# Larger pieces of K work, and a new order for the last heads, in a one-token attention and feed-forward kernel

## The chip, the cores and the metric

The kernel runs on one core of a Trainium2 chip. The metric is the device time of one execution in microseconds (us); lower is better. The six runs of the kernel before lie within 0.33% of each other, so differences of under about 1 us need several runs. The record marks every run used here as fast, that is, undisturbed. The engines are named as in the profile: PE multiplies matrices (PEld is its weight load), DVE is VectorE, ACT is ScalarE, POOL is GpSimd, SP issues nearly all loads. PSUM is the memory into which PE writes its sums. The granted clock is the share of PE's full clock that the profile says PE was given.

## The reference, cut to what matters

```python
x  = A_x                                   # 4 x 1 x 640: one token of four sequences
xn = layernorm(x)
q  = xn @ wq                               # 32 heads of 192
k, v = last W = 2048 positions of the caches, 32 heads     # 4 x 32 x 2048 x 192 each, bf16
o  = softmax(q . k * 192**-0.5) . v
out = x + o @ wo + (silu(xn @ w1) * (xn @ w3)) @ w2
```

Per head the kernel reads 3,072 KB of K and as much of V, once. All inputs together are 222.96 MB, and there is hardly any arithmetic per byte.

## The kernel before

Per head, DVE multiplies K with q in four quarters (`mult`), PE adds up six blocks of 32 columns with identity matmuls (`adder`), and DVE reduces the rest to scores (`reduce_quarter`). Then comes the chain of the head: maximum per partition (`lmax`), transposition on PE, maximum per sequence (`gmax`), broadcast on PE (`bc`), exponential on ACT, and `z`, the exponentials spread for the value product. `pv` is the value product, `ge_sum` gathers it into `po`, `ge_tot` the sum of the exponentials.

```python
def mult(u):                       # u counts quarters: head h = u // 4
    pr = ppool.tile([P, JQ, Dh], BF16, tag="pr")          # 4 buffers
    nc.vector.tensor_tensor(out=pr[:], in0=kts[h][:, g*JQ:(g+1)*JQ, :], in1=<q, repeated>, op=ALU.mult)
def adder(u):
    ps = ps_add.tile([P, JQ, DD], FP32, tag="ps")         # PSUM, 2 buffers, one quarter each
    for kk in range(NK):
        nc.tensor.matmul(ps[:], lhsT=idb[:], rhs=pr[:, :, kk*DD:(kk+1)*DD], start=..., stop=...)
def reduce_quarter(u):
    nc.vector.tensor_reduce(out=scs[h][:, g*JQ:(g+1)*JQ], in_=pss.pop(u)[:], axis=AX.X, op=ALU.add)
...
mt = ps_m.tile([P, P + 1], FP32, tag="mt")                # a PSUM tile of its own for the chain
po = ps_po.tile([P, Dh + 1], FP32, name="po")             # another for ge_sum and ge_tot
...
ends = {H - 2: (NU - 1, NU), H - 1: (NU + 3, NU + 4)}     # slots of pv and ge_sum of the last heads
for h in range(H):
    u0, ul = h * GQ, h * GQ + GQ - 1
    ...
    for u in range(u0, ul + 1):
        add(u, 1, mult, u); add(u + 1, 2, adder, u); add(u + 1, 8, reduce_quarter, u)
    add(ul + 1, 9, chain_lmax, h)
    add(ul + 2, 3, chain_tr, h);  add(ul + 2, 4, chain_gmax, h)
    add(ul + 3, 3, chain_bc, h);  add(ul + 3, 4, chain_z, h)
    add(ul + 4, 5, ge_tot, h)
```

`add(slot, phase, ...)` fixes the order in which each engine gets its instructions. Engines take them in this order, and an instruction that waits holds up those behind it (in a_undo30 below, adder matmuls on PE stand behind a wait of 1.58 us). In before, a head's chain is thus laced into the multiplications of the next head.

Of the kernel before, what the change touches and what calls it, by code (L numbers as in the profile page):

```python
# [10 lines left out]
FP32 = mybir.dt.float32  # L11
# [39 lines left out]
def kernel(  # L51
# [16 lines left out]
    PBUFS: int = 4,  # L68
# [43 lines left out]
    ps_m = ctx.enter_context(tc.tile_pool(name="ps_m", bufs=1, space=MemoryType.PSUM))  # L112
    ps_t = ctx.enter_context(tc.tile_pool(name="ps_t", bufs=1, space=MemoryType.PSUM))
# [7 lines left out]
    wos, o_sbs, rsums, rts, chs, oTs = {}, {}, {}, {}, {}, {}  # L121
# [36 lines left out]
    ones_ff = const.tile([1, 1], FP32, name="ones_ff")  # L158
    nc.vector.memset(ones_ff[:], 1.0)
# [4 lines left out]
    nc.vector.tensor_copy(out=mask_b[:], in_=mask_f[:])  # L164
# [32 lines left out]
    xnT_ps = ps_t.tile([P, KC, B], BF16, tag="t")  # L197
# [11 lines left out]
    xm = ppool.tile([B, 2, PH, 2], BF16, tag="pr", name="xm")  # L209
    nc.gpsimd.memset(xm[:], 0.0)  # L210
    for i in range(2):
        nc.vector.tensor_copy(out=xm[:, i, :, i], in_=xn[:, KM * P:LB])
    xe = ppool.tile([B, 3 + LE, LF], BF16, tag="pr", name="xe")
    nc.gpsimd.memset(xe[:], 0.0)
    for g in range(2):
        b0 = LB + g * 2 * LP
        nc.vector.tensor_copy(out=xe[:, 0:2, g * CT:g * CT + LP].rearrange("b s (e i) -> b s e i", i=LI),
                              in_=xn[:, b0:b0 + 2 * LP].rearrange("b (i e s) -> b s e i", e=LE, s=2))
    nc.vector.tensor_copy(out=xe[:, 2, 0:LP].rearrange("b (e i) -> b e i", i=LI),
                          in_=xn[:, LB + 4 * LP:LB + 5 * LP].rearrange("b (i e) -> b e i", e=LE))  # L220
    for e in range(LE):
        nc.vector.tensor_copy(out=xe[:, 3 + e, CT + e * LI:CT + (e + 1) * LI], in_=xn[:, LB + 5 * LP:D])
    NX = KM + 2
    xw_ps = ps_t.tile([P, NX + 3 + LE, B], BF16, tag="t", name="xw_ps")
    for kc in range(KM):
        nc.tensor.transpose(out=xw_ps[:, kc, :], in_=xn[:, kc:KM * P:KM], identity=idb[0:B, 0:B])
    for i in range(2):
        nc.tensor.transpose(out=xw_ps[:, KM + i, :], in_=xm[:, i].rearrange("b r h -> b (r h)"), identity=idb[0:B, 0:B])
    for i in range(3 + LE):
        nc.tensor.transpose(out=xw_ps[0:LF, NX + i, :], in_=xe[:, i, :], identity=idb[0:B, 0:B])  # L230
    xw = const.tile([P, NX, NREP, B], BF16, name="xw")
    nc.vector.tensor_copy(out=xw[:], in_=xw_ps[:, 0:NX, :].unsqueeze(2).to_broadcast([P, NX, NREP, B]))
    xl = const.tile([LF, 3 + LE, NREP, B], BF16, name="xl")
    nc.vector.tensor_copy(out=xl[:], in_=xw_ps[0:LF, NX:, :].unsqueeze(2).to_broadcast([LF, 3 + LE, NREP, B]))


    qbc = const.tile([P, H * Dh], BF16, name="qbc")
    for c0 in range(0, NQ, 6):
        qps = [pool.tile([P, QC], FP32, tag=tag, name="qps")
               for pool, tag in ((ps_add, "ps"), (ps_add, "ps"), (ps_o, "o_ps"), (ps_o, "o_ps"), (ps_m, "mt"), (ps_t, "t"))]  # L240
        for kc in range(KC):
            for i, qp in enumerate(qps):
                nc.tensor.matmul(qp[:], lhsT=xnT[:, kc].rearrange("p a b -> p (a b)"),  # L243
                                 rhs=wq_rows[kc][:, (c0 + i) * QC:(c0 + i + 1) * QC],
                                 start=(kc == 0), stop=(kc == KC - 1))
# [24 lines left out]
    po = ps_po.tile([P, Dh + 1], FP32, name="po")  # L270
# [3 lines left out]
    def mult(u):  # L274
        h, g = u // GQ, u % GQ
        pr = ppool.tile([P, JQ, Dh], BF16, tag="pr")
        nc.vector.tensor_tensor(out=pr[:], in0=kts[h][:, g * JQ:(g + 1) * JQ, :],  # L277
                                in1=qbc[:, h * Dh:(h + 1) * Dh].unsqueeze(1).to_broadcast([P, JQ, Dh]),
                                op=ALU.mult)
        prs[u] = pr  # L280
        if g == GQ - 1:
            kts.pop(h)

    def adder(u):
        ps = ps_add.tile([P, JQ, DD], FP32, tag="ps")
        pr = prs.pop(u)
        for kk in range(NK):
            nc.tensor.matmul(ps[:], lhsT=idb[:], rhs=pr[:, :, kk * DD:(kk + 1) * DD],  # L288
                             start=(kk == 0), stop=(kk == NK - 1))
        pss[u] = ps  # L290

    def reduce_quarter(u):
# [3 lines left out]
        nc.vector.tensor_reduce(out=scs[h][:, g * JQ:(g + 1) * JQ], in_=pss.pop(u)[:], axis=AX.X, op=ALU.add)  # L296
# [6 lines left out]
    def chain_tr(h):  # L303
        mt = ps_m.tile([P, P + 1], FP32, tag="mt")
# [269 lines left out]
```

## Time and profile before

| | before |
|---|---|
| time, median | 525.69 us (six runs, 525.56 to 527.29; of the first three, 525.79) |
| span of the profile | 523.8 us |
| loads | 222.96 MB, 99.2% of 16 engines' span |
| busy PE, DVE | 69%, 65% |

The first fence is from the page of the kernel before: the engines' busy time, then 40 equal slices of the span (busy share in tenths, and GB/s), then the queue that carries the loads.

```profile
span 523.8 us, 4820 instructions
...
PE 361.8 (69%) x2336; PEld 75.9 (14%) x1643; DVE 340.9 (65%) x413; ACT 55.8 (11%) x176; POOL 5.6 (1%) x12
...
DMA  9999999999999999999999999999999999999996
GB/s 389 422 443 425 433 431 432 428 433 432 430 435 428 437 418 446 424 437 426 434 434 429 432 434 429 435 427 435 425 437 434 427 437 431 430 434 425 441 418 275
...
q1 hardware_dynamic: 11868, 222.96, 99.2%
```

DMA is at 9 in every slice but the last. The slices carry about 431 GB/s. The Trainium skill, "DMA: Bandwidth & Descriptors", section "Where 436 GB/s comes from", gives 435.2 GB/s as the ceiling of the ports of on-chip memory, and the trace stays just under it. The same section expects loads from HBM, as these are, to be held to about 358 GB/s; the 431 GB/s measured here, with one core loading, are above that, so the measurement decides. The loads' 99.2% is 519.6 us: a floor.

Next, three groups of the kernel before, by line and shape: count, then busy us and mean ns of one, then the engine's idle time just before them and what ended it.

```profile
L277 DVE TENSOR_TENSOR pr<-kt,qbc 128x3072 bf16<-128x3072 bf16 x128 | 223.5, 1746 | 104.0 <-DMA kt<-in_A_k_cache_dram 104.0
...
L296 DVE TENSOR_REDUCE sc<-ps 128x16 f32<-128x512 f32 x128 | 87.1, 681 | 2.7 <-PE ps L288 2.6
...
L332 DVE TENSOR_TENSOR z<-ex,mask_b 128x256 bf16<-128x256 bf16 x32 | 13.5, 423 | 38.6 <-ACT ex L324 38.6
```

DVE waited 104.0 us for K to land: it was ahead of the loads. Last, the timeline of the end of before: start us, duration, engine, line, operation; in brackets the idle time before it and its releaser.

```profile
496.99 1.76 DVE L277 TENSOR_TENSOR pr<-kt,qbc 128x3072 bf16<-128x3072 bf16 x1 [4.05 <-DMA kt<-in_A_k_cache_dram]
...
505.17 0.43 DVE L332 TENSOR_TENSOR z<-ex,mask_b 128x256 bf16<-128x256 bf16 x1 [1.44 <-ACT ex L324]
...
506.11 1.75 DVE L277 TENSOR_TENSOR pr<-kt,qbc 128x3072 bf16<-128x3072 bf16 x1
...
510.13 0.22 DVE L300 TENSOR_REDUCE lmax<-sc 128x1 f32<-128x64 f32 x1
...
513.30 2.71 PE L340 MATMUL o_ps<-vt,z 128*8 128x384 bf16 x32 [0.24 <-DVE z L332]
...
516.05 0.48 ACT L343 COPY o_sb<-o_ps 128x384 f32<-128x384 f32 x1 [3.27 <-PE o_ps L340]
...
519.21 0.98 PE L264 MATMUL acc<-wo_t,oT 128*4 128x320 bf16 x12 [0.47 <-DMA wo_t<-in_A_wo_dram]
...
520.38 0.71 PE L264 MATMUL acc<-w,hT 128*4 128x320 bf16 x8 [0.19 <-DMA w<-in_B_w_dram]
```

Head 31's K lands at 496.99 us, and its first multiplication starts at once. Its fourth waits behind head 30's `z` (505.17). The chain's `lmax` is at 510.13, the value product runs from 513.30 to 516.01. The output projection then waits 0.47 us for its weights and the last eight matmuls wait 0.19 us for w2: the loads end last.

### The profile page before, as it was taken

The numbers are of one execution on the slowest core, as the hardware profiler recorded it, in microseconds if no ns is written. First come the engines' busy times: TensorE is split into PE (matmuls) and PEld (weight loads), VectorE is DVE, ScalarE is ACT, GpSimd is POOL, SyncE is SP. The second block draws the span as 40 slices with busy tenths as digits, with TensorE's granted clock in tenths as the row PEclk, the third lists the DMA queues.
The fourth block names the chain that finished last, engine by engine and source line by source line (L and its number), as shares of the span: only waits on it lengthen the run. The fifth ranks groups of instructions, "written<-read, shape, count | busy, mean of one in ns | idle before, by whom it ended". The sixth has DMA issues, their size and how long they took to land.

```text
span 523.8 us, 4820 instructions
## 1 busy us (share of the span) xinstructions
PE 361.8 (69%) x2336; PEld 75.9 (14%) x1643; DVE 340.9 (65%) x413; ACT 55.8 (11%) x176; POOL 5.6 (1%) x12
## 2 busy tenths in 40 slices
PE   0965866887668776667547768586686876675685
PEld 0100111121111111111111111111111111111122
DVE  3268853687656767577646877466667766667671
ACT  2111111111001110101100111001101110011111
POOL 4000000000000000000000000000000000000000
PEclk9979886898878998789997988889878898889988
DMA  9999999999999999999999999999999999999996
GB/s 389 422 443 425 433 431 432 428 433 432 430 435 428 437 418 446 424 437 426 434 434 429 432 434 429 435 427 435 425 437 434 427 437 431 430 434 425 441 418 275
DMA packets 11904, 223.26 MB, mean 426 GB/s; under 512 B 1332, under 2 KB 1608, under 8 KB 3052
## 3 DMA queue, kind: packets, MB, share of 16 engines
q1 hardware_dynamic: 11868, 222.96, 99.2%
q8 instruction: 15, 0.25, 0.2%
q14 instruction: 5, 0.04, 0.0%
q10 hardware_dynamic: 16, 0.01, 0.0%
HBM read 222.96 MB, written 0.01 MB: 426 GB/s over the span
## 4 chain that ended last, share of the span: by engine, by line
DMA 60%; PE 20%; DVE 15%; ACT 3%; issue 1%; SPq 1%
DMA kt<-in_A_k_cache_dram 44%; PE ps L288 11%; DMA w<-in_B_w_dram 11%; DVE pr L277 10%; DMA vt<-in_A_v_cache_dram 5%; PE po L361 4%; PE qps L243 3%; DVE sc L296 2%; ACT ex L324 1%; DVE z L332 1%; DMA x_sb<-in_A_x_dram 1%; PE mt L318 1%; ACT L324 0%; ACT negm L321 0%; PE mt L305 0%
## 5 line engine op out<-in xcount | busy, mean ns | idle before, releaser
L288 PE MATMUL ps<-pr,idb 128*128 128x512 bf16 x768 | 214.7, 422 | 137.6 <-DVE pr L277 137.5
L277 DVE TENSOR_TENSOR pr<-kt,qbc 128x3072 bf16<-128x3072 bf16 x128 | 223.5, 1746 | 104.0 <-DMA kt<-in_A_k_cache_dram 104.0
L296 DVE TENSOR_REDUCE sc<-ps 128x16 f32<-128x512 f32 x128 | 87.1, 681 | 2.7 <-PE ps L288 2.6
L340 PE MATMUL o_ps<-vt,z 128*8 128x384 bf16 x1024 | 60.5, 380 | 0.2 <-DVE z L332 0.2
L361 PE MATMUL po<-o_sb,sel_w 128*32 128x192 f32 x128 | 49.2, 518 | 0.6 <-ACT o_sb L343 0.6
L340 PEld LDWEIGHTS <-z 128*8 128x8 bf16 x1024 | 26.2, 95 | 98.8 <-issue 89.2
L332 DVE TENSOR_TENSOR z<-ex,mask_b 128x256 bf16<-128x256 bf16 x32 | 13.5, 423 | 38.6 <-ACT ex L324 38.6
L343 ACT COPY o_sb<-o_ps 128x384 f32<-128x384 f32 x32 | 15.3, 478 | 196.9 <-PE o_ps L340 196.9
L313 ACT ACTIVATE gneg<-gmax 1x128 f32<-1x128 f32 x32 | 9.8, 308 | 162.8 <-DVE gmax L310 162.8
L305 PEld LDWEIGHTS mt<-idf,lmax 128*1 128x1 f32 x32 | 3.2, 101 | 127.5 <-issue 125.5
L361 PEld LDWEIGHTS po<-o_sb,sel_w 128*32 128x32 f32 x128 | 13.8, 130 | 29.4 <-issue 27.9
L288 PEld LDWEIGHTS <-idb 128*128 128x128 bf16 x124 | 12.0, 97 | 39.3 <-issue 32.8
L318 PEld LDWEIGHTS mt<-ones_ff,gneg 1*128 1x128 f32 x64 | 9.6, 186 | 47.1 <-issue 43.7
L243 PE MATMUL qps<-wt,xnT 128*128 128x512 bf16 x59 | 14.9, 412 | 0.1
L318 PE MATMUL mt<-ones_ff,gneg 1*128 1x1 f32 x64 | 12.3, 259 | 0.7 <-ACT gneg L313 0.7
L321 ACT COPY negm<-mt 128x1 f32<-128x1 f32 x32 | 5.1, 159 | 70.4 <-PE mt L318 70.4
L310 DVE TENSOR_REDUCE gmax<-mt 1x4 f32<-1x128 f32 x32 | 8.8, 274 | 5.8 <-PE mt L305 5.8
L348 PEld LDWEIGHTS po<-rsum,tot_w 128*32 128x32 f32 x64 | 4.4, 108 | 51.5 <-ACT ex L324 35.4
L249 DVE CAST qbc<-qps 128x512 bf16<-128x512 f32 x6 | 3.8, 684 | 11.7 <-PE qps L243 11.7
L324 ACT ACTIVATE ex<-sc,negm 128x64 bf16<-128x64 f32 x32 | 11.1, 348 | 1.0
L305 PE MATMUL mt<-idf,lmax 128*1 128x128 f32 x32 | 10.9, 340 | 0.0
L199 PE MATMUL xnT_ps<-idb,xn 4*128 4x4 bf16 x5 | 0.4, 178 | 13.4 <-DVE xn L194 13.4
(74 smaller groups left out, 84.4 us busy)
## 6 DMA issues: line engine op xcount, KB each, us to landing
kt<-in_A_k_cache_dram SPq DMA_DIRECT2D x32, 3072.0 KB, 19.1
vt<-in_A_v_cache_dram SPq DMA_DIRECT2D x32, 3072.0 KB, 25.5
wo_t<-in_A_wo_dram SPq DMA_DIRECT2D x8, 960.0 KB, 20.7
wt<-in_A_wq_dram SPq DMA_DIRECT2D x2, 3072.0 KB
w<-in_B_w_dram SPq DMA_DIRECT2D x1, 1920.0 KB
wt<-in_A_wq_dram SPq DMA_DIRECT2D x1, 1536.0 KB, 19.5
w<-in_B_w_dram SPq DMA_DIRECT2D x1, 1536.0 KB
w<-in_B_w_dram SPq DMA_DIRECT2D x2, 640.0 KB
```

What stands on the lines that cost most here:

```text
L243: nc.tensor.matmul(qp[:], lhsT=xnT[:, kc].rearrange("p a b -> p (a b)"), rhs=wq_rows[kc][:, (c0 + i) * QC:(c0 + i + 1) * QC], start=(kc == ...
L277: nc.vector.tensor_tensor(out=pr[:], in0=kts[h][:, g * JQ:(g + 1) * JQ, :], in1=qbc[:, h * Dh:(h + 1) * Dh].unsqueeze(1).to_broadcast([P, ...
L288: nc.tensor.matmul(ps[:], lhsT=idb[:], rhs=pr[:, :, kk * DD:(kk + 1) * DD], start=(kk == 0), stop=(kk == NK - 1))
L296: nc.vector.tensor_reduce(out=scs[h][:, g * JQ:(g + 1) * JQ], in_=pss.pop(u)[:], axis=AX.X, op=ALU.add)
L305: nc.tensor.transpose(out=mt[0:1, 0:P], in_=chs[h][0][:], identity=idf[:])
L313: nc.scalar.activation(out=gneg[:], in_=gmax[:].unsqueeze(1).to_broadcast([1, PB, B]), func=ACTF.Copy, scale=-SCALE)
L318: nc.tensor.matmul(mt[:, P:P + 1], lhsT=gneg[:].rearrange("o p b -> o (p b)"), rhs=ones_ff[:], start=True, stop=True)
L324: nc.scalar.activation(out=ex[:], in_=scs.pop(h)[:], func=ACTF.Exp, bias=negm[:, 0:1], scale=SCALE, accum_out=rsum[:])
L332: nc.vector.tensor_tensor(out=z[:], in0=ex[:].unsqueeze(2).to_broadcast([P, NJ, B]), in1=mask_b[:].unsqueeze(1).to_broadcast([P, NJ, B]), ...
L340: nc.tensor.matmul(o_ps[c * CT:c * CT + 2 * B, :], lhsT=z[:, 2 * jj:2 * jj + 2, :], rhs=vt[:, 2 * jj:2 * jj + 2, :], start=(jj < 4), stop= ...
L343: nc.scalar.copy(out=o_sb[:], in_=o_ps[:])
L361: nc.tensor.matmul(po[sl, 0:Dh], lhsT=sel_w[:, par].rearrange("p a b -> p (a b)"), rhs=o_sb[:, par * Dh:(par + 1) * Dh].rearrange("p (r i) ...
```

## The change

The intent: fewer and larger instructions (half heads for heads 0 to 30, quarters only for head 31), and at the end the work of heads 29 and 30 out of the way before head 31 begins, so that head 31's chain is short. The totals of the exponentials are taken once per four heads. To make room in PSUM for pairs of quarters, `mt` and `po` move into one tile. Preparations for w1 move to GpSimd and to later. The core of the diff:

```diff
+    po_mt = ps_po.tile([P, Dh + 1 + P + 1], FP32, name="po_mt")
+    po, mt = po_mt[:, 0:Dh + 1], po_mt[:, Dh + 1:]
+    def mult(u, n):                      # n quarters at once
+        if u % 2 == 0:
+            prs[u] = ppool.tile([P, 2 * JQ, Dh], BF16, tag="pr", name="pr")   # 2 buffers
...
+    def adder(u, n):
+        if u % 2 == 0:
+            pss[u] = ps_add.tile([P, 2, JQ, DD], FP32, tag="ps", name="ps")   # a pair of quarters
...
-    def ge_tot(h):
-        nc.tensor.matmul(po[sl, Dh:Dh + 1], lhsT=<tot_w>, rhs=rsums.pop(h)[:], ...)
+    def ge_mask(hg):  ...  nc.vector.tensor_tensor(out=rw[:], in0=<tot_w>, in1=<four sums>, op=ALU.mult)
+    def ge_tot(hg):   ...  nc.tensor.matmul(po[:, Dh:Dh + 1], lhsT=<rw>, rhs=ones_ff[:], ...)
...
-    ends = {H - 2: (NU - 1, NU), H - 1: (NU + 3, NU + 4)}
+    ends = {H - 3: (NU - 5, NU - 4.9), H - 2: (NU - 1, NU), H - 1: (NU + 3, NU + 4)}
...
+        n = 2 if h < H - 1 else 1
+        for u in range(u0, ul + 1, n):
+            s = u + n if h != H - 2 else u + 1
+            add(u, 1, mult, u, n); add(s, 2, adder, u, n); add(s, 8, reduce_d, u, n)
+        a, b, c = (ul + 1, ul + 2, ul + 3) if h != H - 2 else (ul, ul + 0.1, ul + 0.2)
+        add(a, 9, chain_lmax, h)
+        add(b, 3, chain_tr, h);  add(b, 4, chain_gmax, h)
+        add(c, 3, chain_bc, h);  add(c, 4, chain_z, h)
         if h % HG == HG - 1:
+            add(ul + 4, 4, ge_mask, h // HG)
+            add(ul + 4, 5, ge_tot, h // HG)       # on PE: ahead of pv of head 31
```

The order of the loads is the same in both kernels.

More of the change, by code (lines that the diff above doesn't have):

```diff
@@ L67 @@
     VBUFS: int = 3,
-    PBUFS: int = 4,
+    PBUFS: int = 2,
     L: int = 8,
@@ L111 @@
     ps_o = ctx.enter_context(tc.tile_pool(name="ps_o", bufs=2, space=MemoryType.PSUM))
-    ps_m = ctx.enter_context(tc.tile_pool(name="ps_m", bufs=1, space=MemoryType.PSUM))
-    ps_t = ctx.enter_context(tc.tile_pool(name="ps_t", bufs=1, space=MemoryType.PSUM))
     ps_po = ctx.enter_context(tc.tile_pool(name="ps_po", bufs=1, space=MemoryType.PSUM))
@@ L120 @@
     kts, vts, prs, pss, scs, exs, zs = {}, {}, {}, {}, {}, {}, {}
-    wos, o_sbs, rsums, rts, chs, oTs = {}, {}, {}, {}, {}, {}
+    wos, o_sbs, rsums, rws, rts, chs, oTs = {}, {}, {}, {}, {}, {}, {}
     def load_k(h):
@@ L157 @@
     make_identity(nc, idf[:])
-    ones_ff = const.tile([1, 1], FP32, name="ones_ff")
-    nc.vector.memset(ones_ff[:], 1.0)
+    ones_ff = const.tile([P, 1], FP32, name="ones_ff")
+    nc.gpsimd.memset(ones_ff[:], 1.0)
     mask_f = const.tile([P, B], FP32, name="mask_f")
@@ L163 @@
     mask_b = const.tile([P, B], BF16, name="mask_b")
-    nc.vector.tensor_copy(out=mask_b[:], in_=mask_f[:])
+    nc.gpsimd.tensor_copy(out=mask_b[:], in_=mask_f[:])
     rows = const.tile([P, 2 * B], FP32, name="rows")
@@ L170 @@
     tot_w = head.tile([P, NREP, B], FP32, name="tot_w")
-    nc.vector.tensor_copy(out=tot_w[:], in_=mask_f[:].unsqueeze(1).to_broadcast([P, NREP, B]))
+    nc.gpsimd.tensor_copy(out=tot_w[:], in_=mask_f[:].unsqueeze(1).to_broadcast([P, NREP, B]))
     sel_w = const.tile([P, 2, NREP, B], FP32, name="sel_w")
     for par in range(2):
-        nc.vector.tensor_copy(out=sel_w[:, par], in_=rows[:, par * B:(par + 1) * B].unsqueeze(1).to_broadcast([P, NREP, B]))
+        nc.gpsimd.tensor_copy(out=sel_w[:, par], in_=rows[:, par * B:(par + 1) * B].unsqueeze(1).to_broadcast([P, NREP, B]))
     xf = ppool.tile([B, D], FP32, tag="pr")
@@ L194 @@
     nc.vector.tensor_scalar_mul(out=xn[:], in0=xc[:], scalar1=rstd[:, 0:1])
-    xnT_ps = ps_t.tile([P, KC, B], BF16, tag="t")
+    xnT_ps = ps_add.tile([P, KC, B], BF16, tag="ps")
     for kc in range(KC):
@@ L208 @@
     assert D - LB == 5 * LP + LI and F % LE == 0
-    xm = ppool.tile([B, 2, PH, 2], BF16, tag="pr", name="xm")
-    nc.gpsimd.memset(xm[:], 0.0)
-    for i in range(2):
-        nc.vector.tensor_copy(out=xm[:, i, :, i], in_=xn[:, KM * P:LB])
-    xe = ppool.tile([B, 3 + LE, LF], BF16, tag="pr", name="xe")
-    nc.gpsimd.memset(xe[:], 0.0)
-    for g in range(2):
-        b0 = LB + g * 2 * LP
-        nc.vector.tensor_copy(out=xe[:, 0:2, g * CT:g * CT + LP].rearrange("b s (e i) -> b s e i", i=LI),
-                              in_=xn[:, b0:b0 + 2 * LP].rearrange("b (i e s) -> b s e i", e=LE, s=2))
@@ L219 @@
-    nc.vector.tensor_copy(out=xe[:, 2, 0:LP].rearrange("b (e i) -> b e i", i=LI),
-                          in_=xn[:, LB + 4 * LP:LB + 5 * LP].rearrange("b (i e) -> b e i", e=LE))
-    for e in range(LE):
-        nc.vector.tensor_copy(out=xe[:, 3 + e, CT + e * LI:CT + (e + 1) * LI], in_=xn[:, LB + 5 * LP:D])
-    NX = KM + 2
-    xw_ps = ps_t.tile([P, NX + 3 + LE, B], BF16, tag="t", name="xw_ps")
-    for kc in range(KM):
-        nc.tensor.transpose(out=xw_ps[:, kc, :], in_=xn[:, kc:KM * P:KM], identity=idb[0:B, 0:B])
@@ L227 @@
-    for i in range(2):
-        nc.tensor.transpose(out=xw_ps[:, KM + i, :], in_=xm[:, i].rearrange("b r h -> b (r h)"), identity=idb[0:B, 0:B])
-    for i in range(3 + LE):
-        nc.tensor.transpose(out=xw_ps[0:LF, NX + i, :], in_=xe[:, i, :], identity=idb[0:B, 0:B])
-    xw = const.tile([P, NX, NREP, B], BF16, name="xw")
-    nc.vector.tensor_copy(out=xw[:], in_=xw_ps[:, 0:NX, :].unsqueeze(2).to_broadcast([P, NX, NREP, B]))
-    xl = const.tile([LF, 3 + LE, NREP, B], BF16, name="xl")
-    nc.vector.tensor_copy(out=xl[:], in_=xw_ps[0:LF, NX:, :].unsqueeze(2).to_broadcast([LF, 3 + LE, NREP, B]))
@@ L237 @@
     qbc = const.tile([P, H * Dh], BF16, name="qbc")
     for c0 in range(0, NQ, 6):
-        qps = [pool.tile([P, QC], FP32, tag=tag, name="qps")
-               for pool, tag in ((ps_add, "ps"), (ps_add, "ps"), (ps_o, "o_ps"), (ps_o, "o_ps"), (ps_m, "mt"), (ps_t, "t"))]
+        pairs = [ps_add.tile([P, 2, QC], FP32, tag="ps", name="qps") for _ in range(2)]
+        qps = [pair[:, i, :] for pair in pairs for i in range(2)]
+        qps += [ps_o.tile([P, QC], FP32, tag="o_ps", name="qps")[:] for _ in range(2)]
@@ L241 @@
         for kc in range(KC):
             for i, qp in enumerate(qps):
-                nc.tensor.matmul(qp[:], lhsT=xnT[:, kc].rearrange("p a b -> p (a b)"),
+                nc.tensor.matmul(qp, lhsT=xnT[:, kc].rearrange("p a b -> p (a b)"),
                                  rhs=wq_rows[kc][:, (c0 + i) * QC:(c0 + i + 1) * QC],
@@ L248 @@
             if i % 2:
-                nc.vector.tensor_copy(out=dst, in_=qp[:])
+                nc.vector.tensor_copy(out=dst, in_=qp)
             else:
-                nc.scalar.copy(out=dst, in_=qp[:])
+                nc.scalar.copy(out=dst, in_=qp)
     o_banks = []
@@ L268, in acc_add, with reduce_d @@
             acc_half(i, lhsT, rhs, last=last)
-    po = ps_po.tile([P, Dh + 1], FP32, name="po")
+    po_mt = ps_po.tile([P, Dh + 1 + P + 1], FP32, name="po_mt")
+    po, mt = po_mt[:, 0:Dh + 1], po_mt[:, Dh + 1:]
     def x_add(i):
         acc_half(i, idb[0:B, 0:B], x_sb, first=True)
-    def mult(u):
+    def mult(u, n):
         h, g = u // GQ, u % GQ
-        pr = ppool.tile([P, JQ, Dh], BF16, tag="pr")
-        nc.vector.tensor_tensor(out=pr[:], in0=kts[h][:, g * JQ:(g + 1) * JQ, :],
-                                in1=qbc[:, h * Dh:(h + 1) * Dh].unsqueeze(1).to_broadcast([P, JQ, Dh]),
-                                op=ALU.mult)
-        prs[u] = pr
-        if g == GQ - 1:
-            kts.pop(h)
-    def adder(u):
-        ps = ps_add.tile([P, JQ, DD], FP32, tag="ps")
-        pr = prs.pop(u)
-        for kk in range(NK):
-            nc.tensor.matmul(ps[:], lhsT=idb[:], rhs=pr[:, :, kk * DD:(kk + 1) * DD],
-                             start=(kk == 0), stop=(kk == NK - 1))
-        pss[u] = ps
-    def reduce_quarter(u):
+        if u % 2 == 0:
+            prs[u] = ppool.tile([P, 2 * JQ, Dh], BF16, tag="pr", name="pr")
+        i = (u % 2) * JQ
+        nc.vector.tensor_tensor(out=prs[u - u % 2][:, i:i + n * JQ, :], in0=kts[h][:, g * JQ:(g + n) * JQ, :],
+                                in1=qbc[:, h * Dh:(h + 1) * Dh].unsqueeze(1).to_broadcast([P, n * JQ, Dh]),
+                                op=ALU.mult)
+    def adder(u, n):
+        if u % 2 == 0:
+            pss[u] = ps_add.tile([P, 2, JQ, DD], FP32, tag="ps", name="ps")
+        ps, pr = pss[u - u % 2], prs[u - u % 2]
+        for i in range(u % 2, u % 2 + n):
+            for kk in range(NK):
+                nc.tensor.matmul(ps[:, i], lhsT=idb[:], rhs=pr[:, i * JQ:(i + 1) * JQ, kk * DD:(kk + 1) * DD],
+                                 start=(kk == 0), stop=(kk == NK - 1))
+    def reduce_d(u, n):
         h, g = u // GQ, u % GQ
@@ L295, in reduce_quarter @@
             scs[h] = small.tile([P, NJ], FP32, tag="sc", name="sc")
-        nc.vector.tensor_reduce(out=scs[h][:, g * JQ:(g + 1) * JQ], in_=pss.pop(u)[:], axis=AX.X, op=ALU.add)
+        nc.vector.tensor_reduce(out=scs[h][:, g * JQ:(g + n) * JQ],
+                                in_=pss[u - u % 2][:, u % 2:u % 2 + n].rearrange("p i j d -> p (i j) d"),
+                                axis=AX.X, op=ALU.add)
     def chain_lmax(h):
@@ L303, in chain_tr @@
     def chain_tr(h):
-        mt = ps_m.tile([P, P + 1], FP32, tag="mt")
         nc.tensor.transpose(out=mt[0:1, 0:P], in_=chs[h][0][:], identity=idf[:])
-        chs[h].append(mt)
     def chain_gmax(h):
         gmax = small.tile([1, B], FP32, tag="gmax")
-        nc.vector.tensor_reduce(out=gmax[:], in_=chs[h][1][0:1, 0:P].rearrange("o (p b) -> o b p", b=B),
+        nc.vector.tensor_reduce(out=gmax[:], in_=mt[0:1, 0:P].rearrange("o (p b) -> o b p", b=B),
                                 axis=AX.X, op=ALU.max)
@@ L316, in chain_bc @@
     def chain_bc(h):
-        lmax, mt, gneg = chs[h]
-        nc.tensor.matmul(mt[:, P:P + 1], lhsT=gneg[:].rearrange("o p b -> o (p b)"), rhs=ones_ff[:],
+        lmax, gneg = chs.pop(h)
+        nc.tensor.matmul(mt[:, P:P + 1], lhsT=gneg[:].rearrange("o p b -> o (p b)"), rhs=ones_ff[0:1, :],
                          start=True, stop=True)
@@ L321, in chain_bc @@
         nc.scalar.copy(out=negm[:], in_=mt[:, P:P + 1])
-        rsum = small.tile([P, 1], FP32, tag="rsum", bufs=4)
+        if h % HG == 0:
+            rsums[h // HG] = small.tile([P, HG], FP32, tag="rsum", bufs=2, name="rsum")
         ex = small.tile([P, NJ], BF16, tag="ex")
         nc.scalar.activation(out=ex[:], in_=scs.pop(h)[:], func=ACTF.Exp, bias=negm[:, 0:1], scale=SCALE,
-                             accum_out=rsum[:])
-        rsums[h] = rsum
+                             accum_out=rsums[h // HG][:, h % HG:h % HG + 1])
         exs[h] = ex
@@ L344, in pv, with ge_mask, ge_tot @@
         o_sbs[h] = o_sb
-    def ge_tot(h):
-        sl = slice((h % HG) * CT, (h % HG + 1) * CT)
-        nc.tensor.matmul(po[sl, Dh:Dh + 1], lhsT=tot_w[:].rearrange("p a b -> p (a b)"), rhs=rsums.pop(h)[:],
+    def ge_mask(hg):
+        rw = small.tile([P, HG, CT], FP32, tag="rw", bufs=1, name="rw")
+        nc.vector.tensor_tensor(out=rw[:], in0=tot_w[:].rearrange("p a b -> p (a b)").unsqueeze(1).to_broadcast([P, HG, CT]),
+                                in1=rsums.pop(hg)[:].unsqueeze(2).to_broadcast([P, HG, CT]), op=ALU.mult)
+        rws[hg] = rw
+    def ge_tot(hg):
+        nc.tensor.matmul(po[:, Dh:Dh + 1], lhsT=rws.pop(hg)[:].rearrange("p h c -> p (h c)"), rhs=ones_ff[:],
                          start=True, stop=True)
-        chs.pop(h)
     def ge_rec(hg):
@@ L382, with w1_rows, w1_x @@
     ffn = {}
+    NX = KM + 2
+    xw = const.tile([P, NX, NREP, B], BF16, name="xw")
+    xl = const.tile([LF, 3 + LE, NREP, B], BF16, name="xl")
+    xs = {}
+    def w1_rows():
+        xm = small.tile([B, 2, PH, 2], BF16, tag="xm", bufs=1, name="xm")
+        nc.gpsimd.memset(xm[:], 0.0)
+        for i in range(2):
+            nc.gpsimd.tensor_copy(out=xm[:, i, :, i], in_=xn[:, KM * P:LB])
+        xe = small.tile([B, 3 + LE, LF], BF16, tag="xe", bufs=1, name="xe")
+        nc.gpsimd.memset(xe[:], 0.0)
+        for g in range(2):
+            b0 = LB + g * 2 * LP
+            nc.gpsimd.tensor_copy(out=xe[:, 0:2, g * CT:g * CT + LP].rearrange("b s (e i) -> b s e i", i=LI),
+                                  in_=xn[:, b0:b0 + 2 * LP].rearrange("b (i e s) -> b s e i", e=LE, s=2))
+        nc.gpsimd.tensor_copy(out=xe[:, 2, 0:LP].rearrange("b (e i) -> b e i", i=LI),
+                              in_=xn[:, LB + 4 * LP:LB + 5 * LP].rearrange("b (i e) -> b e i", e=LE))
+        for e in range(LE):
+            nc.gpsimd.tensor_copy(out=xe[:, 3 + e, CT + e * LI:CT + (e + 1) * LI], in_=xn[:, LB + 5 * LP:D])
+        xs.update(m=xm, e=xe)
+    def w1_x():
+        xm, xe = xs["m"], xs["e"]
+        xw_ps = ps_add.tile([P, NX + 3 + LE, B], BF16, tag="ps", name="xw_ps")
+        for kc in range(KM):
+            nc.tensor.transpose(out=xw_ps[:, kc, :], in_=xn[:, kc:KM * P:KM], identity=idb[0:B, 0:B])
+        for i in range(2):
+            nc.tensor.transpose(out=xw_ps[:, KM + i, :], in_=xm[:, i].rearrange("b r h -> b (r h)"), identity=idb[0:B, 0:B])
+        for i in range(3 + LE):
+            nc.tensor.transpose(out=xw_ps[0:LF, NX + i, :], in_=xe[:, i, :], identity=idb[0:B, 0:B])
+        nc.vector.tensor_copy(out=xw[:], in_=xw_ps[:, 0:NX, :].unsqueeze(2).to_broadcast([P, NX, NREP, B]))
+        nc.vector.tensor_copy(out=xl[:], in_=xw_ps[0:LF, NX:, :].unsqueeze(2).to_broadcast([LF, 3 + LE, NREP, B]))
     FM, FH = KM * F, KM * F + F // 2
@@ L408, in w1_in @@
         wt, we = ffn["w1"], ffn["w1e"]
-        ps = ffn["ps"] = ps_t.tile([P, FW], FP32, tag="t", name="f_ps")
+        ps = ffn["ps"] = ps_add.tile([P, FW], FP32, tag="ps", name="f_ps")
         def mm(w, lhsT, rhs, c0=0, start=False, stop=False):
@@ L442, in w3_in @@
     def w3_in():
-        ffn["ps"] = ps_t.tile([P, FW], FP32, tag="t", name="f_ps")
+        ffn["ps"] = ps_add.tile([P, FW], FP32, tag="ps", name="f_ps")
         for kc in range(KC):
@@ L485 @@
             add(u0 + 2, 0, load_v, h)
-        for u in range(u0, ul + 1):
-            add(u, 1, mult, u)
-            add(u + 1, 2, adder, u)
-            add(u + 1, 8, reduce_quarter, u)
-        add(ul + 1, 9, chain_lmax, h)
-        add(ul + 2, 3, chain_tr, h)
-        add(ul + 2, 4, chain_gmax, h)
-        add(ul + 3, 3, chain_bc, h)
-        add(ul + 3, 4, chain_z, h)
-        add(ul + 4, 5, ge_tot, h)
+        n = 2 if h < H - 1 else 1
+        for u in range(u0, ul + 1, n):
+            s = u + n if h != H - 2 else u + 1
+            add(u, 1, mult, u, n)
+            add(s, 2, adder, u, n)
+            add(s, 8, reduce_d, u, n)
+        a, b, c = (ul + 1, ul + 2, ul + 3) if h != H - 2 else (ul, ul + 0.1, ul + 0.2)
+        add(a, 9, chain_lmax, h)
+        add(b, 3, chain_tr, h)
+        add(b, 4, chain_gmax, h)
+        add(c, 3, chain_bc, h)
+        add(c, 4, chain_z, h)
         if h % HG == HG - 1:
+            add(ul + 4, 4, ge_mask, h // HG)
+            add(ul + 4, 5, ge_tot, h // HG)
             add(ul + 4, 9, ge_rec, h // HG)
@@ L511 @@
         add(4 + 2 * n, 1, w1_low, n)
+    add(5, 0, w1_rows)
+    add(9, 7, w1_x)
     add(13, 7, w1_in)
```

## The prediction

> **What bounds the kernel now.** The load queue. The page's queue table gives queue q1 99.2% of 16 engines' span: 519.6 of 523.8 us for 222.96 MB, all of which must be read. The slices show DMA at 9 in every slice but the last, while PE is busy 69% and VectorE 65%. The Trainium skill, "DMA: Bandwidth & Descriptors", section "Where 436 GB/s comes from", puts the ceiling at 435.2 GB/s; the slices here show about 431, so the trace agrees and hardly any rate is left to win.
>
> The chain of waits for the last 40 us says the same: V load from 465.17 to 489.66, then the last w2 chunks, issued from 489.7 to 497.3 us, landing at 520.34; then eight acc matmuls (0.76 us), the cast (0.47 us) and the store, to 523.8. Everything is queued by 497.3 us, so from there the end is set by bytes alone.
>
> **What the change does to each engine.**
> - VectorE: 31 heads use two multiplications of 6144 columns instead of four of 3072 (1746 ns each), and two reductions instead of four (681 ns each). The work per element stays; 62 starts of each kind go. Small VectorE operations here take 0.14 to 0.2 us, so I estimate 0.05 to 0.1 us saved per start: 6 to 12 us of 341. Eight mask products are added (about 0.3 us each, estimated from the 128x256 z product at 0.42), 2.4 us. About 1 us of w1 row copies goes to GpSimd.
> - PE: the totals go from 64 matmul records (7.1 us) to 16: about 5 us of 362. Adder and value matmuls stay.
> - Head: the w1 transposes (about 1 us) move behind the q product, which starts about 1 us earlier. The first V load, issued at 26.2 us when a wq buffer frees, may go out earlier, but 14.2 MB (33 us at 431 GB/s) are queued ahead of it: no gain.
> - Tail: head 30's chain and head 29's value product go ahead of head 31's multiplications. In before, head 31's fourth multiplication waits until 506.1 us behind head 30's z at 505.2. Head 31's compute should end 1 to 3 us earlier (its o_sb copy was at 516.05). But the last projection already waited 0.47 us for wo_t, and the last acc matmuls for w2.
>
> **On the critical path:** nothing of it, within about 0.2 us. K loads may go out some us earlier or later, but when K is issued at 477.99 us, the K before it still lands at 482.4 and V at 489.7: over 10 us of queue is in hand.
>
> **Predicted time:** 525.6 us against 525.79; range 524.5 to 527.0. Faster by over 2%: 0.01; within 2%: 0.98; slower by over 2%: 0.01.
>
> **What would show each step right.** Queue q1 still about 519.6 us of engine time and DMA 9 throughout; the last w2 landing within 0.5 us of 520.3, the rest after it again about 3.5 us; VectorE busy 328 to 338 us; head 31's o_sb copy at 513 to 515.5 us, followed by longer PE waits on wo_t and w2; first q matmul near 14 us instead of 15.15.
>
> **What would make it wrong.** A stretch where the queue runs dry: the w1 and w3 products now borrow an adder buffer, and GpSimd writes what the w1 transposes read, so PE could stop for a while in the first 110 us; a K or V load issued over 10 us late costs the excess one for one. Or a final chain of head 31 that ends after 520.3 us: its totals now pass a mask product after the exponential.

## The result, and the profile after

The changed kernel takes 533.45 us (median of six runs, 531.49 to 534.12), against 525.69 us. The ratio is 1.0135, 95% interval 1.0113 to 1.0157: 1.35% slower. That is within the 2% to which the prediction gave 0.98, but far outside its range, which ended at 527.0 us. Ratios here and below are the mean time of one kernel's fast runs over that of the other's of the same rounds, so not quite the ratio of the medians quoted.

The same lines of the page of the changed kernel:

```profile
span 530.1 us, 4584 instructions
...
PE 364.1 (69%) x2288; PEld 65.7 (12%) x1534; DVE 334.0 (63%) x284; ACT 55.9 (11%) x176; POOL 7.5 (1%) x25
...
DMA  9999999999999999999999999999999999999991
GB/s 386 430 430 430 437 428 428 435 430 431 431 430 436 433 428 434 430 432 433 433 430 432 430 433 427 436 432 431 430 433 426 436 430 436 434 424 439 426 421 72
...
q1 hardware_dynamic: 11868, 222.96, 98.1%
```

98.1% of 530.1 us is 520.0 us: the loads take what they took. Only the last slice lost: 72 GB/s instead of 275. For the w2 chunks, the profile says how long after its issue a load landed:

```profile
DMA to landing us min/median/max: 23.8/27.2/30.6
```

The last two are issued at 489.64 and 496.9 us and land 30.6 and 23.8 us later, at 520.2 and 520.7; in before it was 520.3 and 520.8. The queue never ran dry, and PE did not wait for w2 at all. The time is lost after the loads. The groups of the changed kernel, by line and shape:

```profile
L251 DVE TENSOR_TENSOR pr<-kt,qbc 128x6144 bf16<-128x6144 bf16 x62 | 207.1, 3341 | 28.9 <-DMA kt<-in_A_k_cache_dram 28.9
L268 DVE TENSOR_REDUCE sc<-ps 128x32 f32<-128x1024 f32 x62 | 75.5, 1217 | 11.8 <-PE ps L261 11.8
...
L304 DVE TENSOR_TENSOR z<-ex,mask_b 128x256 bf16<-128x256 bf16 x32 | 13.5, 422 | 82.6 <-ACT ex L297 82.6
```

VectorE's busy time fell as intended, from 340.9 to 334.0 us. But it waited for K only 28.9 us instead of 104.0, and `z` waited for the exponential 82.6 us instead of 38.6. It does less work and is less ahead of the loads. That alone costs nothing: in a_undo30_mt_tot_ps below, which is as fast as before, the same two waits are 46.3 and 75.0 us. Here is the end of the changed kernel, as a timeline:

```profile
481.43 0.54 SPq L123 DMA_DIRECT2D kt<-in_A_k_cache_dram  x1
...
486.19 2.76 PE L261 MATMUL ps<-pr,idb 128*128 128x512 bf16 x12 [0.57 <-DVE pr L251]
...
490.44 3.33 DVE L251 TENSOR_TENSOR pr<-kt,qbc 128x6144 bf16<-128x6144 bf16 x1
...
493.83 4.45 PE L261 MATMUL ps<-pr,idb 128*128 128x512 bf16 x12 [2.48 <-DVE pr L251]
...
498.32 1.22 DVE L268 TENSOR_REDUCE sc<-ps 128x32 f32<-128x1024 f32 x1 [4.21 <-PE ps L261]
499.58 0.22 DVE L274 TENSOR_REDUCE lmax<-sc 128x1 f32<-128x64 f32 x1
...
500.68 1.52 PE L337 MATMUL po_mt<-o_sb,sel_w 128*32 128x192 f32 x4 [0.46 <-DVE gmax L282]
...
503.20 0.42 DVE L304 TENSOR_TENSOR z<-ex,mask_b 128x256 bf16<-128x256 bf16 x1 [2.68 <-ACT ex L297]
503.55 3.42 DVE L251 TENSOR_TENSOR pr<-kt,qbc 128x3072 bf16<-128x3072 bf16 x2
...
515.63 0.22 DVE L274 TENSOR_REDUCE lmax<-sc 128x1 f32<-128x64 f32 x1
...
519.09 0.55 PE L325 MATMUL po_mt<-ones_ff,rw 128*128 128x1 f32 x2 [1.47 <-DVE rw L320]
...
519.57 2.73 PE L312 MATMUL o_ps<-vt,z 128*8 128x384 bf16 x32
...
522.35 0.48 ACT L315 COPY o_sb<-o_ps 128x384 f32<-128x384 f32 x1 [4.07 <-PE o_ps L312]
...
526.72 0.71 PE L235 MATMUL acc<-w,hT 128*4 128x320 bf16 x8
```

The first line is the issue of head 31's K. The view of that line and time gives its landing:

```profile
DMA to landing us min/median/max: 15.5/15.5/15.5
```

So head 31's K was there at 496.9 us, but its first multiplication starts at 503.55. Before it come head 30's second half (490.44) with its 12 adder matmuls (493.83, 4.45 us), their reduction (498.32), and the whole chain of head 30 from `lmax` (499.58) to `z` (503.20), with the `ge_sum` of head 29 (500.68) in the middle of it on PE. Meanwhile DVE mostly waits. Part of this lateness is the granted clock: the 12 adder matmuls of head 30's first half took 2.76 us (486.19), those of its second half 4.45, with a granted clock of 0.71 between 495 and 500 us. No run holds the clock fixed, so what these 1.7 us are worth is not shown. The last matmuls with w2 come at 526.72 us. The account of the two profiles, from the lines shown:

| piece | before | after | difference |
|---|---|---|---|
| start of head 31's multiplications | 496.99 | 503.55 | +6.56 |
| from there to `lmax` of head 31 | 13.14 | 12.08 | -1.06 |
| from `lmax` to the end of the value product | 5.88 | 6.67 | +0.79 |
| from there to the end of the span | 7.79 | 7.80 | +0.01 |
| sum | | | +6.30 (530.1 - 523.8) |

So 6.6 us of wait came in, only 1.1 us came back because head 30's chain is no longer laced into head 31 (its value product, at 511.99, still is), and 0.8 us is the totals: in before they were done while `z` was computed, now a mask product after `z` and their matmul both stand ahead of the value product. The profiled run is one of the faster ones of the changed kernel (531.97 us); the difference of the medians is 7.8 us.

### The profile page after: what moved, and what is told of

It reads as the page before. It is cut to its first block, busy times and chain, and to the rows that moved or that the text cites. A ratio compares the mean times of both kernels' runs of the same rounds, so it can differ in the third digit from the quotient of the medians.

```text
span 530.1 us, 4584 instructions
## 1 busy us (share of the span) xinstructions
PE 364.1 (69%) x2288; PEld 65.7 (12%) x1534; DVE 334.0 (63%) x284; ACT 55.9 (11%) x176; POOL 7.5 (1%) x25
## 3 DMA queue, kind: packets, MB, share of 16 engines
q1 hardware_dynamic: 11868, 222.96, 98.1%
## 4 chain that ended last, share of the span: by engine, by line
DMA 51%; DVE 27%; PE 18%; ACT 1%; issue 1%; SPq 0%
DMA kt<-in_A_k_cache_dram 43%; DVE pr L251 18%; PE ps L261 9%; DMA w<-in_B_w_dram 5%; DVE sc L268 5%; DMA wt<-in_A_wq_dram 4%; PE po_mt L337 3%; PE o_ps L312 2%; PE qps L214 1%; PE po_mt L278 1%; DVE gmax L282 1%; PE acc L235 1%; DVE z L304 1%; DVE lmax L274 1%; ACT ex L297 1%
## 5 line engine op out<-in xcount | busy, mean ns | idle before, releaser
L261 PE MATMUL ps<-pr,idb 128*128 128x512 bf16 x768 | 220.2, 447 | 18.7 <-DVE pr L251 16.8
L251 DVE TENSOR_TENSOR pr<-kt,qbc 128x6144 bf16<-128x6144 bf16 (+1 forms) x66 | 214.0, 3245 | 28.9 <-DMA kt<-in_A_k_cache_dram 28.9
L268 DVE TENSOR_REDUCE sc<-ps 128x32 f32<-128x1024 f32 (+1 forms) x66 | 78.2, 1185 | 14.5 <-PE ps L261 14.5
L278 PE MATMUL po_mt<-idf,lmax 128*1 128x128 f32 x32 | 9.6, 301 | 94.5 <-DVE lmax L274 94.5
L304 DVE TENSOR_TENSOR z<-ex,mask_b 128x256 bf16<-128x256 bf16 x32 | 13.5, 422 | 82.6 <-ACT ex L297 82.6
L337 PE MATMUL po_mt<-o_sb,sel_w 128*32 128x192 f32 x128 | 48.7, 515 | 14.1 <-DVE gmax L282 12.5
L312 PE MATMUL o_ps<-vt,z 128*8 128x384 bf16 x1024 | 51.5, 336 | 0.0
L290 PEld LDWEIGHTS po_mt<-ones_ff,gneg 1*128 1x128 f32 x64 | 9.4, 182 | 106.7 <-issue 105.8
L282 DVE TENSOR_REDUCE gmax<-po_mt 1x4 f32<-1x128 f32 x32 | 8.9, 279 | 16.4 <-PE po_mt L278 16.4
L337 PEld LDWEIGHTS po_mt<-o_sb,sel_w 128*32 128x32 f32 x128 | 14.0, 130 | 35.3 <-issue 29.5
L290 PE MATMUL po_mt<-ones_ff,gneg 1*128 1x1 f32 x64 | 12.1, 256 | 0.7 <-ACT gneg L285 0.7
```

What stands on the lines that cost most here:

```text
L251: nc.vector.tensor_tensor(out=prs[u - u % 2][:, i:i + n * JQ, :], in0=kts[h][:, g * JQ:(g + n) * JQ, :], in1=qbc[:, h * Dh:(h + 1) * Dh].u ...
L261: nc.tensor.matmul(ps[:, i], lhsT=idb[:], rhs=pr[:, i * JQ:(i + 1) * JQ, kk * DD:(kk + 1) * DD], start=(kk == 0), stop=(kk == NK - 1))
L268: nc.vector.tensor_reduce(out=scs[h][:, g * JQ:(g + n) * JQ], in_=pss[u - u % 2][:, u % 2:u % 2 + n].rearrange("p i j d -> p (i j) d"), ax ...
L278: nc.tensor.transpose(out=mt[0:1, 0:P], in_=chs[h][0][:], identity=idf[:])
L282: nc.vector.tensor_reduce(out=gmax[:], in_=mt[0:1, 0:P].rearrange("o (p b) -> o b p", b=B), axis=AX.X, op=ALU.max)
L290: nc.tensor.matmul(mt[:, P:P + 1], lhsT=gneg[:].rearrange("o p b -> o (p b)"), rhs=ones_ff[0:1, :], start=True, stop=True)
```

## The experiments

Theory A: the reordering puts head 30's chain between the landing of head 31's K and its use, and half heads make that chain late. Rival B: half heads alone make the stream of K work lag. Rival C: the reordering costs in any granularity. Each experiment's name says its base: `a_` starts from the changed kernel, `b_` from the kernel before. Every result was correct.

| run | median us | ratio to before | 95% interval |
|---|---|---|---|
| changed kernel | 533.45 | 1.0135 | 1.0113 to 1.0157 |
| a_undo30 | 527.85 | 1.0038 | 1.0021 to 1.0055 |
| b_order | 525.83 | 1.0002 | 0.9987 to 1.0017 |
| a_q30 | 530.80 | 1.0091 | 1.0076 to 1.0106 |
| a_lag30 | 530.96 | 1.0095 | 1.0080 to 1.0110 |
| a_undo30_totlate | 526.90 | 1.0026 | 1.0007 to 1.0045 |
| a_undo30_mt | 526.59 | 1.0011 | 0.9999 to 1.0024 |
| a_undo30_mt_tot | 525.60 | 0.9995 | 0.9983 to 1.0008 |
| a_mt | 531.22 | 1.0102 | 1.0089 to 1.0114 |
| a_q30_mt_tot | 528.39 | 1.0052 | 1.0032 to 1.0072 |
| a_lag30_mt_tot | 529.01 | 1.0055 | 1.0042 to 1.0068 |
| a_q30_mt_tot_ps | 525.59 | 0.9999 | 0.9985 to 1.0012 |
| a_undo30_mt_tot_ps | 525.59 | 0.9993 | 0.9981 to 1.0006 |

### a_undo30: the reordering taken back

```diff
-    ends = {H - 3: (NU - 5, NU - 4.9), H - 2: (NU - 1, NU), H - 1: (NU + 3, NU + 4)}
+    ends = {H - 2: (NU - 1, NU), H - 1: (NU + 3, NU + 4)}
-            s = u + n if h != H - 2 else u + 1
+            s = u + n
-        a, b, c = (ul + 1, ul + 2, ul + 3) if h != H - 2 else (ul, ul + 0.1, ul + 0.2)
+        a, b, c = ul + 1, ul + 2, ul + 3
```

> The changed kernel, with only the reordering for heads 29 and 30 undone (half heads, totals per four heads and the rest stay). Theory A (the loss is head 30's chain standing, finished late because of half heads, between the landing of head 31's K and its first multiplication): head 31's first multiplication starts at its K's landing near 497.5 us again, head 31's last multiplication ends near 508 us, and the time is 525.5 to 527 us. Rival B (half heads make the whole stream of K work lag, VectorE waits for K only 15 times instead of 29, so the last head is late whatever the order): still 531 us or more.

Measured: 527.85 us. Most of the loss, 5.6 us by the medians, is gone, and rival B falls as the main cause; but the time lies 0.9 us above the range, so 2.1 us had another cause. The timeline of a_undo30, whose profiled run is the fastest of its four (526.65 us), shows where to look:

```profile
496.96 1.76 DVE L251 TENSOR_TENSOR pr<-kt,qbc 128x3072 bf16<-128x3072 bf16 x1 [0.82 <-DMA kt<-in_A_k_cache_dram]
...
502.11 1.52 PE L337 MATMUL po_mt<-o_sb,sel_w 128*32 128x192 f32 x4 [1.58 <-DVE gmax L282]
...
515.06 0.35 PE L325 MATMUL po_mt<-ones_ff,rw 128*128 128x1 f32 x2 [1.48 <-DVE rw L320]
```

Head 31 starts when its K lands again. But inside head 31, `ge_sum` of head 29 waits 1.58 us for head 30's `gmax`, because DVE multiplies first, and the adder matmuls stand behind it. In before, `ge_sum` did not wait for `gmax` (no wait is given in its line); the two used different PSUM tiles:

```profile
500.82 1.55 PE L361 MATMUL po<-o_sb,sel_w 128*32 128x192 f32 x4
```

The third line of a_undo30 is the totals' matmul, which stands between the mask product and the value product.

### b_order: the reordering alone, on the kernel before

```diff
+            s = u + 1 if (h, u) != (H - 2, ul) else ul + 0.05
+            add(s, 2, adder, u); add(s, 8, reduce_quarter, u)
+        a, b, c = (ul + 1, ul + 2, ul + 3) if h != H - 2 else (ul + 0.05, ul + 0.1, ul + 0.2)
```

(with the `ends` of the changed kernel)

> The kernel before, with only the reordering for heads 29 and 30 (quarters throughout, totals per head). Theory A: head 30's last quarter needs one adder group of 6 matmuls (1.5 us) instead of 12, its chain ends near 498.7 us, head 31's first multiplication starts 1 to 2 us after its K lands, and what head 30's z no longer takes inside head 31 pays for that: 525.3 to 526.5 us. Rival C (the reordering costs by itself, whatever the pieces): 529 us or more.

Measured: 525.83 us, ratio 1.0002. Rival C falls: with quarters the same order costs nothing that can be told from noise. The timeline of b_order:

```profile
492.90 1.46 PE L288 MATMUL ps<-pr,idb 128*128 128x512 bf16 x6 [0.27 <-DVE pr L277]
...
498.61 3.42 DVE L277 TENSOR_TENSOR pr<-kt,qbc 128x3072 bf16<-128x3072 bf16 x2
...
516.08 0.48 ACT L343 COPY o_sb<-o_ps 128x384 f32<-128x384 f32 x1 [2.76 <-PE o_ps L340]
```

Head 30's last group is six matmuls of 1.46 us instead of twelve of 4.45, and head 31 starts at 498.61 instead of 503.55. Its `o_sb` copy comes at 516.08, against 516.05 in before: even here the reordering only moves the wait and gains nothing.

### a_q30 and a_lag30: head 30's chain made earlier inside the changed kernel

```diff
 a_q30:
-        n = 2 if h < H - 1 else 1
+        n = 2 if h < H - 2 else 1       # head 30 in quarters, the last one at slot ul + 0.05
 a_lag30:
-            s = u + n if h != H - 2 else u + 1
+            s = u + n if (h, u) != (H - 2, ul - 1) else ul
```

> The changed kernel, with head 30 in quarters too; the reordering stays. Theory A: head 30's chain ends 3 to 5 us earlier, head 31's first multiplication starts near 499 to 500 us instead of 503.6, and the time falls by 3 to 5 us, to 527 to 530 us. Rival B: no change, 531 us or more.

> The changed kernel, but the sums of head 30's first half go behind the multiplication of its second half (one slot of lag, as in all other heads), so this multiplication no longer waits for PE's 12 adder matmuls and their reduction. Theory A: it starts near 487.7 us instead of 490.4, and the time falls by 2 to 3 us. If the step that costs is only the chain after it, or rival B holds, the time changes by under 1 us.

Measured: 530.80 us for a_q30, 0.8 us above its range, with head 31's first multiplication at 502.14, not near 500: quarters alone do not make head 30's chain as early as in b_order. a_lag30 met its expectation: 530.96 us, 2.5 us less, and the second half's multiplication at 487.83. Head 31's start in a_q30, then in a_lag30:

```profile
502.14 3.42 DVE L251 TENSOR_TENSOR pr<-kt,qbc 128x3072 bf16<-128x3072 bf16 x2
500.54 3.42 DVE L251 TENSOR_TENSOR pr<-kt,qbc 128x3072 bf16<-128x3072 bf16 x2
```

So the lateness of head 30's chain counts, but not one for one: head 31 starts 1.41 and 3.01 us earlier than in the changed kernel, and the medians fall by 2.65 and 2.49 us. The granted clock differs too: between 500 and 510 us it is 0.66 and 0.54 in these profiles, 0.83 in the changed kernel's. And half heads are not all that makes the chain late.

### a_undo30_totlate, a_undo30_mt, a_undo30_mt_tot: what is left without the reordering

```diff
 totlate:
-            add(ul + 4, 5, ge_tot, h // HG)
+            add(ul + 4, 5 if h < H - 1 else 8, ge_tot, h // HG)      # behind pv of head 31
 mt:
-    po_mt = ps_po.tile([P, Dh + 1 + P + 1], FP32, name="po_mt")
-    po, mt = po_mt[:, 0:Dh + 1], po_mt[:, Dh + 1:]
+    po = ps_po.tile([P, Dh + 1], FP32, name="po")
+    # mt of head h: columns 384 to 511 of the value product's tile h % 2
```

The third run, `mt_tot`, has both edits. Theory D: what is left of the loss is the place of the totals and the PSUM tile that `po` and `mt` share. Rival B': it is half heads or the lower granted clock.

> As a_undo30 (reordering undone, 527.85 us, 2.1 us above the kernel before), and for the last four heads the totals' matmul goes behind head 31's value product on PE instead of ahead of it. In a_undo30 z ends near 514.6 us, but the value product starts only at 515.35 us, behind the mask product and the totals. Theory D (what is left of the loss is 0.7 us of totals and 1.2 us of PE waiting for gmax, because po and mt now share one PSUM tile): 0.5 to 0.8 us less, 527.0 to 527.4 us. Rival B' (what is left comes from half heads or from the lower granted clock, 0.857 against 0.892): no change, 527.6 us or more.

> As a_undo30, but mt no longer shares a PSUM tile with po: it lies behind the value sums' columns in their two tiles. In a_undo30 the sum over heads (ge_sum) waits for gmax 30 times, 14.8 us in all, the last time 1.58 us at 502.1 us inside head 31. Theory D: these waits go, head 31's second adder group starts near 502.3 instead of 503.56 us, and 1.0 to 1.3 us less, 526.5 to 526.9 us. Rival B': no change, 527.6 us or more.

> Both edits on top of a_undo30: half heads for heads 0 to 30 and the other parts of the change stay. Theory D: the compute ends again before the last load, the time is that of the kernel before within 0.1%, 525.4 to 526.2 us, with a granted clock still near 0.857. Rival B': 526.8 us or more.

Measured: 526.90, 526.59 and 525.60 us; by the ratios 0.6, 1.4 and 2.3 us less than a_undo30. The first lies 0.1 us below its range, the other two are as expected. The totals' share alone is not clear of noise (the intervals overlap), that of `mt` is barely so (they share only 1.0021 to 1.0024); both together are: a_undo30_mt_tot is the same as the kernel before. It keeps half heads for heads 0 to 30 and has a mean granted clock of 0.857 in its profile, like the changed kernel's 0.855. So neither half heads nor the lower mean clock cost time by themselves. Theory D holds.

### a_mt: only mt moved, the reordering kept

Its edit is the `mt` edit above, on the changed kernel.

> The changed kernel with its reordering, only mt out of po's PSUM tile. In it ge_sum waited for gmax 0.46 us at 489.5 and again at 500.7 us, the second time inside head 30's chain ahead of head 31. Theory A with D: 0.5 to 1.2 us less than the changed kernel's 533.45, 532.2 to 533 us; the reordering keeps costing over 5 us. If the shared tile were the main cause instead of the order: under 529 us.

Measured: 531.22 us, 1 us below the range; the order still costs most of the loss. Its profiled run (532.28 us, the slowest of its five) starts head 31 only at 504.49 us and again has head 30's adder group at 4.45 us, so the profile does not show where the extra 1 us came from. That stays open.

### a_q30_mt_tot and a_lag30_mt_tot: the reordering kept, the two waits removed

> The changed kernel with its reordering kept, head 30 in quarters (a_q30: 530.8 us), mt out of po's PSUM tile and the last totals behind the value product. In a_q30 the reordered quarters still ran late: PE waited 1.58 us for gmax at 487.6 us, and z of head 30 ended at 502.1 us, against 498.6 in b_order. Theory A with D (reordering costs only when head 30's chain is late, through half heads or through the shared tile): z of head 30 ends near 499 us, and the time is 525.5 to 527.5 us. If the reordering costs by itself inside the changed kernel: 529 us or more.

> The changed kernel with its reordering kept and half heads kept for head 30, but with the lag of a_lag30 (530.96 us), mt out of po's tile and the last totals behind the value product. Theory A with D: the chain of head 30 still stands behind a whole half head's 12 adder matmuls, so z of head 30 ends near 500 us, 3 us after head 31's K landed; 528 to 530 us, between a_lag30 and the kernel before. Under 527 us would say that half heads cost nothing here and the shared tile and totals were all.

Measured: 528.39 and 529.01 us. The second is as expected. The first missed its range by 0.9 us, and the two are not clear of each other: with these tiles, quarters for head 30 show no gain over half heads. The timeline of the first, from the slowest of its six runs (530.62 us), names a third wait:

```profile
493.81 1.46 PE L261 MATMUL ps<-pr,idb 128*128 128x512 bf16 x6 [1.24 <-DVE sc L268]
...
504.69 5.28 PE L261 MATMUL ps<-pr,idb 128*128 128x512 bf16 x12 [0.78 <-DVE sc L268]
```

An odd quarter's adder matmuls wait for the reduction of the even quarter, although they write other columns: since the change, two quarters share one PSUM tile. The second line also shows 12 matmuls in 5.28 us, at a granted clock of 0.51 between 500 and 510 us, so two causes were left. The last pair of runs removes the shared tile.

### a_q30_mt_tot_ps and a_undo30_mt_tot_ps: a PSUM tile for each quarter

```diff
-        if u % 2 == 0:
+        if u % n == 0:
             pss[u] = ps_add.tile([P, 2, JQ, DD], FP32, tag="ps", name="ps")
-        ps, pr = pss[u - u % 2], prs[u - u % 2]
+        ps, pr = pss[u], prs[u - u % 2]
                                           # the reduction reads pss[u] too
```

> As a_q30_mt_tot (528.39 us, 0.9 us above what was expected of it), but each quarter's sums of heads 30 and 31 get a PSUM tile of their own. There an odd quarter's adder matmuls waited for the reduction of the even quarter that shares its tile: 1.24 us at 493.8, 0.78 us at 504.7 us; b_order, with a tile for each quarter, waits 0.27 us there. Theory D' (the same kind of wait, for a tile that is shared though the columns are not): head 30's z ends near 498 us, and the time falls by 0.8 to 2 us, to 526.3 to 527.6 us. If those waits are no loss: 528 us or more, and what is left is the granted clock (0.51 from 500 to 510 us in that profile) or the order itself.

> As a_undo30_mt_tot (525.60 us, reordering undone), with a PSUM tile for each quarter of head 31. Its adder group for the last quarter waited 1.24 us for the reduction at 508.4 us. Head 31's value product should end about 1 us earlier, but the loads still land near 520.3 us: 525.2 to 525.8 us, the same as the kernel before within 0.1%. If the loads were not the floor, it would fall to 524.6 us or less.

Measured: 525.59 us for both. The first fell 2.8 us, more than the waits named in its expectation (2.0 us) and to 0.7 us below its range, and is as fast as the kernel before with the reordering kept. From its timeline:

```profile
492.91 1.46 PE L261 MATMUL ps<-pr,idb 128*128 128x512 bf16 x6 [0.36 <-DVE pr L251]
...
498.64 3.42 DVE L251 TENSOR_TENSOR pr<-kt,qbc 128x3072 bf16<-128x3072 bf16 x2
```

Head 31 starts at 498.64, as in b_order (498.61), and 0.74 us earlier than in a_q30_mt_tot (499.38). The stretch from 500 to 510 us, first in a_q30_mt_tot, then here (the third number from the end is the granted clock):

```profile
500.00:510.00 10.00, 8.03 (x22) 0.10 (x8) 7.52 (x6) 0.00 (x0) 0.00 (x0) 0.51 0.99 426
500.00:510.00 10.00, 8.86 (x57) 0.92 (x35) 7.37 (x8) 0.48 (x1) 0.00 (x0) 0.80 0.99 426
```

With the waits the low clock is gone as well (and the first profile is of the slowest of its runs). The edit gave back the 2.8 us; how much of it went through the waits and how much through the clock is not shown. From its page, the loads' queue:

```profile
q1 hardware_dynamic: 11868, 222.96, 99.2%
```

It is at 99.2% again: the loads are the floor. In the second, head 31's value product ends about 1 us earlier than in a_undo30_mt_tot (515.3 us), and the time does not fall. That shows the floor from the other side, and why no version here is clearly faster than the kernel before: the best three, all at 525.6 us, have intervals that include 1.

## Why the prediction was wrong, point by point

- "What bounds the kernel now": right. The loads took 520.0 us of engine time (519.6 before), the last w2 chunks landed at 520.2 and 520.7 us (520.3 and 520.8 before), DMA stayed at 9. The prediction took the floor for the whole answer. A floor tells that the change cannot win; it does not tell that it cannot lose.
- The step that failed is the tail: "Head 31's compute should end 1 to 3 us earlier (its o_sb copy was at 516.05)". The copy came at 522.35, 6.3 us later. The prediction counted what no longer stands inside head 31 (1.06 us came back) and not what now stands in front of it: head 30's 12 adder matmuls, reduction and chain, 6.56 us past the landing of K. In before it could have been estimated: 1.46 us for six adder matmuls, 0.68 us for a reduction, 3.1 us from `lmax` to the end of `z` in head 31's chain; the clock that stretched twelve matmuls to 4.45 us could not. And the gain was not there even where head 30's chain was early: in b_order the copy came at 516.08.
- "On the critical path: nothing of it, within about 0.2 us": wrong for the same reason. The prediction had itself read waits of 0.47 us for wo_t and a short one for w2. It took them as proof that compute was off the path, when they are the size of the slack. "Over 10 us of queue is in hand" was right for the loads and says nothing of the compute behind the last load.
- Shared PSUM tiles were seen only as a risk for w1 and w3 in the first 110 us. They cost in the last head: with the reordering undone, `mt` with `po` 1.4 us by the ratios; with it kept and head 30 in quarters, pairs of quarters 2.8 us (with the change of clock that came with it).
- "What would make it wrong" named a final chain of head 31 ending after 520.3 us, and the mask product in it. That is what happened; the totals are 0.8 us of it. With a range that ended at 527.0, it got too little weight.
- VectorE busy 334.0 us: inside the predicted 328 to 338. PE's totals fell by 3.3 us, not 5: 16 records of 310 ns instead of 64 of 181. The first q matmul came at 13.18 us instead of 15.15, the first V load at 25.70, and neither gave time: right.

What the runs show together: the reordering costs 5.6 us in the changed kernel, 0.1 us (within noise) in the kernel before, and nothing once head 30 is in quarters, the shared tiles are parted and the last totals moved. The cost belongs to the combination. Open are how much of it passes through the granted clock of the last 40 us, the extra 1 us of a_mt, and why runs of the changed kernel spread over 2.6 us.

## What to carry to other kernels

When loads are the floor, ask of every change at the end of the kernel how much compute remains behind the last load and how many tenths of a us it has in hand; then walk that chain instruction by instruction in the new order, the waits that come in as well as those that go out. Putting finished work "out of the way" ahead of the last piece pays only if it really is finished by the time the last piece's data land; here larger pieces were part of what made it late. The Trainium skill, "Perfetto Trace Analysis", section "Optimizing Scalar/DVE Operations", says that breaking instructions up may let work complete sooner where these engines are not saturated but hold up others; here, with VectorE at 63%, the reverse step was taken for heads 0 to 30, and going back to quarters for head 30 restored the time only with a tile for each quarter, `mt` out of `po`'s tile and the last totals moved (a_q30_mt_tot_ps, 525.59 us).

## What the Trainium skill lacked or had wrong

- "PSUM — Partial Sum Buffer", section "PSUM bank collisions raise a hardware error", asks to guard by bank and group of 32 partitions, not by address. `po` and `mt` in one 2 KB bank obey this: PE waited 12.5 us in all for `gmax` in the changed kernel, none in before. By the page's rule most of these waits were not needed: `gmax` reads partition 0, and `ge_sum` of head h writes the group of 32 partitions h % 4; the program guards the whole tile. No run here left the wait out. The page does not say what such packing costs an engine that works in order: 1.4 us at the end of this kernel. For a pair of quarters in one tile of 4 KB (two banks, by the page's 2 KiB each) the wait was the program's, by tile; a tile for each quarter took it away (528.39 to 525.59 us).
- "TensorE: Matmul & The Clock Gate", section "Part 1: The HAM clock gate", says that activity releases the throttle. The trace agrees in kind: a group of 12 adder matmuls took 2.76 us in some places and 4.45 us in others. No page gives a figure for what a change in the size of VectorE's pieces goes with: all runs of kernels with half heads had a mean clock of 0.848 to 0.869, all runs with quarters throughout 0.883 to 0.909. These kernels also differ in the rest of the change, so that the size of the pieces is the cause is not shown. That difference of the mean cost no time here (a_undo30_mt_tot, 0.857, 525.60 us).
- "Perfetto Trace Analysis", section "Optimizing Scalar/DVE Operations", gives about 60 ns of overhead for one VectorE instruction on SBUF and says that the profiled latency holds about twice that. Nothing is wrong here: two multiplications of 3072 columns take 2 x 1746 ns, one of 6144 takes 3341, so 151 ns are saved in the records, near an estimate of 120 ns from the page's figure.
